# The two layers of an attention-and-ELU network on scaled float16 pairs, its first 384 tokens on whole float32 operands

## The chip, the cores and the metric

The kernel runs on one core of one Trainium2 chip, in one launch. The metric is the time of an execution on the device in microseconds; the number given for a kernel is the median of several runs. Engines are named as in the profile: PE is the matrix engine (PEld its weight loads), DVE the vector engine, ACT the scalar engine, POOL the general engine (GpSimd), SP the engine that issues the DMAs.

## What is computed

Causal attention with a decay, for 8 batch elements, 8 heads, 576 tokens and a head size of 64, then two dense layers with an ELU between them on the 4608 tokens of width 512 (2048 hidden units). The reference, cut to what matters:

```python
scores = scale * np.matmul(q, k.transpose(0, 1, 3, 2))
s_pos = np.maximum(s, 0.0)
cum = np.cumsum(s_pos, axis=-1)
bias = -(cum[:, :, :, None] - cum[:, :, None, :])
scores = np.where(causal, -1000000000.0, scores + np.minimum(bias, 0.0))
scores = scores - np.max(scores, axis=-1, keepdims=True)
attn = np.exp(scores)
attn = attn / (np.sum(attn, axis=-1, keepdims=True) + 1e-09)
attn_out = np.matmul(attn, v)
...
x = np.ascontiguousarray(attn_out.transpose(0, 2, 1, 3)).reshape(B * S, H * D)
...
h = x @ w_in
g = np.where(h > 0.0, h, alpha * (np.exp(np.minimum(h, 0.0)) - 1.0))
return (g @ w_out).astype(np.float32)
```

The scale is 1/8, alpha is 1, x is 4608 x 512, w_in 512 x 2048, w_out 2048 x 512. Here s, q, k and v are float32. The two weight matrices arrive with eight bytes an element, and the kernel turns them into float32 on the chip (lines 541 to 552).

## The kernel before, in words

**The planner.** The order of the work is not written out by hand. Every operation is registered with `op` (lines 112 to 152): a priority, one or more ways to do it (an engine and an assumed cost in nanoseconds), what it reads and what it writes. `issue` (lines 161 to 269) then repeats one step until all is issued: among the operations whose inputs are done it takes the one that can start first on its assumed clock, and among equals the one with the lowest priority number, on the engine that would finish it first. Each engine carries out its list in that order, and so does SP with its DMAs. A tile's buffer is one of a few slots under a tag, and a slot is given out in the order in which the tiles were registered.

**Attention.** It is worked through in pieces (lines 1278 and 1279): first the tokens 0 to 319 of the batch elements 0 to 2 ("low" units, lines 608 to 735, twelve of them, on whole float32 operands with transposes on PE), then the elements 3 to 7 with all 576 tokens, then the tokens 320 to 575 of the elements 0 to 2. Beyond the low units there is a unit for each head (`prepare`, `scoring`, `weighing`, lines 737 to 1083) and one for each pair of heads' first 64 tokens. Scores come from float32 operands split in two rounded parts (L882), the softmax goes through DVE (L885), ACT (L890) and DVE again, the probabilities are split into two float16 parts (L935 to L943), turned by a DMA (L369) and multiplied with V in three parts, which PE reads as the upper halves of float32 words (L1013). V is loaded in `values` (lines 845 to 856), or at line 636 for a low unit. The result of each pair of heads goes to a buffer in HBM, `x_dram`.

**The two layers.** The tokens are taken in the order in which attention finishes them, in twelve chunks of 384. Counted from 0, chunk 0 holds the element 0's low tokens and 64 of element 1; chunks 2, 5 and 8 are the first to need the elements 3, 5 and 7; the last two hold the late tokens of the elements 0 to 2. `load_x` (line 1145) loads x of a chunk, transposed, and `moe_chunk` (line 1157) does the rest. Every operand is split into a rounded part (`rounded`, line 372, type float32r, read by PE in one pass) and the rest (`rest`, line 384), so that a product takes three matmuls: high times high, high times low, low times high. That holds for x (lines 1161 to 1167), for both weight matrices (`load_unit`, lines 525 to 562, in 32 pieces of 128 x 512) and for the hidden values. For each of the 16 blocks of 128 hidden units:

- `hidden` (line 1172): 4 x 3 matmuls of 384 columns into PSUM (L1178);
- ACT takes the exponential (L1186); DVE or ACT takes min(.,1) - 1 or its negative (L1195, L1191); DVE joins it with max(h, 0) in PSUM (L1200); ACT or DVE writes the rounded copy (L394, L395); DVE writes the rest (L1203);
- `project` (line 1207), one block later: 3 x 3 matmuls of 512 columns onto three accumulators of 128 tokens (L1216).

At a chunk's end the accumulators are copied out (line 1250) and stored.

**Priorities and slots around the change.** The layers' work on the side engines has priority -1000 plus the chunk's number, ahead of attention; their matmuls have 10000 plus the chunk's number, behind attention. The weights' pieces have `W0 + WD * f` (45 + 5f), among attention's units, which count up in steps of 10 for the low units and 5 after them. A piece as it arrives takes 4 KB of a partition, in one of two slots of the tag "io" or, until x of chunk 0 is split, one of the two slots "xx" of the split x. Its split form stays in its own tile (`w_in_f`, `w_out_f`) for the whole kernel.

## Time and profile before

| | |
|---|---|
| runs, median | 1125.65 us (1124.69 to 1129.84, 3 runs) |
| profiled execution, first to last instruction (its span, the one time that the page gives for it) | 1121.7 us |
| instructions in it | 19900 |
| PE busy | 1098.8 us, 6069 matmul records |
| DVE, ACT, POOL busy | 842.3, 627.1, 448.5 us |
| moved by DMA | 156.52 MB, 140 GB/s mean |
| first matmul of the layers | at 87.15 us |
| last write of x to HBM issued | at 968.9 us |

The profile is one execution, taken by the hardware. Its page gives the busy time of each engine, the granted clock of PE in tenths of full speed, and the chain of work that ended last. The groups' rows read: line, engine, operation, output<-inputs, partitions x elements of output and inputs, count | busy us, mean ns of one | idle time of the engine just before them, and what ended it. PEld rows are the weight loads, which run beside the matmuls. A matmul's duration includes filling and draining the array, so consecutive ones overlap, and the time that one takes from the next is the distance of their starts. In a timeline the columns are start (us), length (us), engine, line, operation; equal neighbours are put in one row with their count. A tile's rows give minimum, median and maximum length in ns and the first and last start.

### The profile page before, as it was taken

How to read it: one execution, taken by the hardware profiler on the slowest of the kernel's cores; microseconds unless marked ns; L12 is line 12 of the kernel's file. 1: busy time of each engine (PE TensorE's matmuls, PEld its weight loads, DVE VectorE, ACT ScalarE, POOL GpSimd, SP SyncE). 2: the span in 40 equal slices, each digit the busy share in tenths (PEclk: the TensorE clock that was granted, in tenths of full speed). 3: DMA queues.
4: the chain of work that ended last, by engine and by line, in shares of the span. 5: the costliest groups of instructions: out<-in, count | busy, mean ns of one | idle time of the engine just before them, and what ended most of it. 6: DMA issues, size and time to landing. Idle time of an engine off the chain costs nothing.

```text
span 1121.7 us, 19900 instructions
## 1 busy us (share of the span) xinstructions
PE 1098.8 (98%) x6069; PEld 955.5 (85%) x6069; DVE 842.3 (75%) x2133; ACT 627.1 (56%) x1525; POOL 448.5 (40%) x657
## 2 busy tenths in 40 slices
PE   8999999999999999999999999999999999999998
PEld 7779888888888888888888888888888888899997
DVE  6888999778888887677887887788888888422322
ACT  5887666455556655555565555555655556433433
POOL 7663573345436234344333533445444433100000
PEclk9999999999999999999999999999999999999999
DMA  6976788567666855666755656667787687210000
GB/s 171 274 196 203 183 206 191 124 141 167 154 127 143 175 126 127 153 141 139 158 117 122 162 136 138 145 131 177 167 185 165 138 191 144 51 57 1 29 1 28
DMA packets 341689, 156.52 MB, mean 140 GB/s; under 512 B 266424, under 2 KB 320464, under 8 KB 341584
## 3 DMA queue, kind: packets, MB, share of 16 engines
q1 hardware_dynamic: 341584, 155.27, 59.4%
q8 instruction: 48, 0.79, 0.3%
q14 instruction: 57, 0.47, 0.1%
HBM read 79.66 MB, written 19.32 MB: 88 GB/s over the span
## 4 chain that ended last, share of the span: by engine, by line
PE 73%; DVE 4%; DMA 3%; issue 1%; POOL 1%; ACT 1%; SPq 1%; POOLq 0%; DVEq 0%; ACTq 0%
PE o L1216 29%; PE h L1178 29%; PE av L1013 8%; PE sc L882 6%; DVE p L943 1%; DMA T<-p 1%; DMA stq<-in_qT_dram 1%; DVE p L885 1%; DMA q<-qs 0%; DMA vs<-in_vb_dram 0%; DVE h L1200 0%; DVE xl L387 0%; DMA out_dram<-ost 0%; DMA x_dram<-x 0%; DVE qs L387 0%
## 5 line engine op out<-in xcount | busy, mean ns | idle before, releaser
L1178 PE MATMUL h<-xh,wi 128*128 128x384 f32 x1536 | 444.6, 339 | 1.1 <-DVE gl L1203 1.1
L1216 PE MATMUL o<-wo,gh 128*128 128x512 f32 x1152 | 362.1, 395 | 0.1
L1178 PEld LDWEIGHTS h<-xh,wi 128*128 128x128 f32 x1536 | 282.6, 188 | 9.3 <-DVE gl L1203 2.4
L1178 PE MATMUL h<-xl,wi 128*128 128x384 f32 x768 | 258.4, 336 | 0.0
L1216 PEld LDWEIGHTS o<-wo,gh 128*128 128x128 f32 x1152 | 207.0, 188 | 27.4 <-DVE mn L885 0.5
L1216 PE MATMUL o<-wo,gl 128*128 128x512 f32 x576 | 227.3, 395 | 0.9 <-DVE gl L1203 0.9
L1200 DVE SCALAR_TENSOR_TENSOR h<-h,g 128x384 f32<-128x384 f32 x192 | 107.8, 561 | 121.6 <-ACT g L1191 120.1
L1186 ACT ACTIVATE g<-h 128x384 f32<-128x384 f32 x192 | 94.1, 490 | 175.4 <-PE h L1178 166.0
L890 ACT ACTIVATE p<-p,mn 128x192 f32<-128x192 f32 (+1 forms) x232 | 144.9, 625 | 72.2 <-DVE mn L885 69.1
L943 DVE SCALAR_TENSOR_TENSOR p<-p,sm,p 128x512 f16<-128x512 f32 (+3 forms) x239 | 170.6, 741 | 8.1 <-POOL p L935 4.9
L1178 PEld LDWEIGHTS h<-xl,wi 128*128 128x128 f32 x768 | 144.4, 188 | 6.8
L935 POOL TENSOR_SCALAR p<-p,sm 128x512 f16<-128x512 f32 (+3 forms) x125 | 87.8, 709 | 134.8 <-DVE sm L896 51.8
L394 ACT CAST gh<-h 128x384 fp32r<-128x384 f32 x175 | 83.5, 477 | 86.7 <-DVE h L1200 85.4
L1203 DVE TENSOR_TENSOR gl<-h,gh 128x384 fp32r<-128x384 f32 x192 | 105.8, 551 | 32.8 <-ACT gh L394 31.7
L1216 PEld LDWEIGHTS o<-wo,gl 128*128 128x128 f32 x576 | 108.0, 188 | 25.2 <-DVE gl L1203 1.3
L885 DVE CUSTOM_DVE_ANT_0 p<-sc,maskw 128x192 f32<-128x192 f32 (+1 forms) x232 | 109.7, 482 | 24.9 <-PE sc L882 21.1
L1013 PEld LDWEIGHTS <-vs 128*128 128x128 bf16 x896 | 79.7, 98 | 49.7 <-issue 13.9
L1013 PE MATMUL av<-T,vs 128*128 128x256 f16 (+5 forms) x896 | 119.2, 285 | 2.8 <-DMA T<-p 2.1
L388 POOL TENSOR_TENSOR vs<-vs 128x320 f32<-128x320 f32 x72 | 60.4, 839 | 124.6 <-DMA vs<-in_vb_dram 71.1
L882 PE MATMUL sc<-kh,qs 128*128 128x192 f32 (+2 forms) x272 | 87.2, 325 | 2.1 <-DVE mn L885 1.8
L882 PE MATMUL sc<-k,q 128*128 128x192 f32 (+2 forms) x272 | 83.8, 312 | 1.4 <-POOL k L388 0.9
L1191 ACT ACTIVATE g<-g 128x384 f32<-128x384 f32 x138 | 72.5, 525 | 4.2
(149 smaller groups left out, 1368.7 us busy)
## 6 DMA issues: line engine op xcount, KB each, us to landing
stk<-in_kT_dram SPq DMA_DIRECT2D x64, 288.0 KB
vs<-in_vb_dram SPq DMA_DIRECT2D x64, 160.0 KB
stq<-in_qT_dram SPq DMA_DIRECT2D x40, 256.0 KB
w_i<-in_w_in_dram SPq DMA_DIRECT2D x16, 512.0 KB
w_o<-in_w_out_dram SPq DMA_DIRECT2D x16, 512.0 KB
out_dram<-ost SPq DMA_DIRECT2D x32, 256.0 KB
x_dram<-x_None SPq DMA_DIRECT2D x20, 288.0 KB
q<-qs SPq DMA_DIRECT2D x40, 128.0 KB
```

Of the source, the lines that this page charges most:

```text
L394: ("ACT", act_c(n), lambda: act.copy(dst(), src())),
L882: pe_.matmul(view(sc.v[:, :cw]), l, r, start=n == 0, stop=n == len(pairs) - 1)
L885: op(prio, [("DVE", 84 + dve_p(cw), lambda i=i, sc=sc: dve.tensor_tensor_reduce(pt.v[:, i * cw : (i + 1) * cw], sc.v[:, :cw], mv(i * cw, c ...
L890: op(prio, [("ACT", 480 + w / 1.2, lambda: act.activation(pt.v[:, :w], pt.v[:, :w], AF.Exp, bias=mn.v[:, n - 1 : n], scale=-1.0, accum_out ...
L935: ("Pool", 160 + 1.04 * n, lambda part=part: pool.tensor_scalar(part(t16, 0), own(part), sm.v[:, r], 1.0, ALU.mult, ALU.mult)),
L943: ("DVE-SB", dve_2(n), lambda part=part: dve.scalar_tensor_tensor(part(t16, 1), own(part), sm.v[:, r], part(t16, 0), ALU.mult, ALU.subtract)),
L1013: op(prio, [("PE", cost, lambda m=m, operands=operands, rows=rows: pe_.matmul(av.v[:rows, dst], *operands(), start=first and m == 0, stop= ...
L1178: pe_.matmul(hp.v[:, :TC], w_in_f[f].v[:, part, c * P : (c + 1) * P], xx.v[:, c, :TC], start=(c == 0 and m == 0), stop=(c == NCB - 1 and m ...
L1186: op(side, [("ACT", act_c(TC), lambda: act.activation(g.v[:, :TC], hp.v[:, :TC], AF.Exp))], [hp], [g])
L1200: op(side, [("DVE", dve_p(TC), lambda: dve.scalar_tensor_tensor(hp.v[:, :TC], hp.v[:, :TC], 0.0, g.v[:, :TC], ALU.max, join[0]))], [g], [hp])
L1203: op(side, [("DVE", dve_p(TC), lambda: dve.tensor_tensor(gl.v[:, :TC], hp.v[:, :TC], gh.v[:, :TC].bitcast(F32), ALU.subtract))], [hp, gh], ...
L1216: pe_.matmul(acc[i].v, g.v[:, tb], w_out_f[f].v[:, part], start=(f == 0 and m == 0), stop=(f == NF - 1 and m == 2),)
```

## The change

- **Scales.** For the two weight matrices, for V of the low units together, and for V of every later group of a batch element, the largest absolute value is found on chip: `peak` reduces a tile to one number for each partition (on DVE, or for a weight piece on ACT with an accumulator), and `scales_of` takes the largest over the columns, stores 128 numbers to HBM, loads all of them back into every partition, reduces again, and makes a power of two from the exponent bits. `scales_of` is called nine times: once for the weights with the low V, eight times for the groups. V bounds x, since x is a mean of V's rows.
- **Chunks 1 to 11.** x, the weights and the hidden values are scaled by these powers of two and split into a float16 part and a float16 rest. The three matmuls for each product stay; their operands are float16. The hidden value stays scaled in PSUM: ACT takes the exponential with the scale undone, DVE multiplies by the scale and takes the larger of the two (`max` in place of the sum), the float16 part is a copy times 2**-22, and the rest follows on DVE. The output copy undoes the scale. `chunk_scales` works out five numbers for a chunk with small DVE operations.
- **Chunk 0.** It uses the float32 words of the weights, x as loaded and the hidden value as one float32 tile: one matmul where there were three, no split of x, weights or hidden value.
- **Weights.** A piece's float32 words get a tile of their own (`w_in_f`, `w_out_f`, half the size of before); the float16 pairs (`w_parts`) are made after the scales, by `split_unit`, at priority -500 + f. The rest of a weight is made on DVE only (before: DVE or POOL). Arriving pieces have the two slots "io" alone. The step between the pieces' priorities, `WD`, is 3 (5 before).
- **x.** The split x takes half the space; x of chunk 0 uses the tiles of the later split x instead of "io" slots.

The diff, cut to its core:

```diff
-W0, WD = 45, 5
+W0, WD = 45, 3
...
+    def peak(prio, n, src, reads, at, axis=mybir.AxisListType.X, aside=None, also=()):
+        col = slice(at, at + 1)
+        ways = [("DVE-SB", 100 + 1.04 * n, lambda: dve.tensor_reduce(
+            peaks.v[:, col], src(), axis, ALU.max, apply_absolute_value=True))]
+        if aside is not None:
+            ways.append(("ACT", 480 + n / 1.2, lambda: act.activation(
+                aside(), src(), AF.Abs, accum_out=peaks.v[:, col])))
+        op(prio, ways, reads, [(peaks, at), *also])
...
+    def scales_of(prio, spans, dst):
...
+        used = [(peaks, m) for at, k in spans for m in range(at, at + k)]
+        op(prio, [("DVE-SB", 30.0 + 70 * n, largest)], used, [own])
+        load(prio, lambda: aside.v.rearrange("n p -> p n"), lambda: own.v, [own], [aside], P * n * 4)
+        load(prio, lambda: every.v, lambda: aside.v.rearrange("n p -> (n p)").partition_broadcast(P),
+             [aside], [every], P * P * n * 4)
+        op(prio, [("DVE-SB", 300.0 + 130 * n, exponents)], [every], [own, (scales, dst)])
...
+    def weight_scales():
+        scales_of(-600, [(A_IN, NF + 1), (A_OUT, NF + 1), (A_LOW, N_CUT * NP + 1)], 0)
...
-        raw = plan.buf(sb, shape, dtype, f"w_{n}", tag="io", bufs=N_IO,
-                       others=[("xx", 2, 0)] + [(t, 1, 0) for t in later])
...
+            raw = plan.buf(sb, [P, 512, 2], U32, f"w_{n}", tag="io", bufs=N_IO,
+                           others=[(w.key[1], 1, 0) for w in w_parts[:N_STAGE]], always=True)
...
-        rounded(prio, 512, lambda: parts.v[:, 0], value, [words], [(parts, 0)])
-        rest(prio, 512, lambda: parts.v[:, 1], value, lambda: parts.v[:, 0].bitcast(F32),
-             [words, (parts, 0)], [(parts, 1)])
+        peak(prio, 512, lambda: value.v, [value], (A_IN, A_OUT)[kind] + f,
+             aside=(lambda: raw.v[:, :, 0].bitcast(F32)) if wide else None, also=[(raw, 0)] if wide else [])
+
+    def split_unit(f, kind, value):
+        prio, col, parts = -500 + f, slice(kind, kind + 1), w_parts[f]
+        scaled(prio, 512, lambda: parts.v[:, kind, 0], lambda: value.v, lambda: scales.v[:, col],
+               [value, (scales, 0)], [(parts, (kind, 0))])
+        op(prio, [("DVE-SB", dve_2(512), lambda: dve.scalar_tensor_tensor(
+            parts.v[:, kind, 1], value.v, scales.v[:, col], parts.v[:, kind, 0], ALU.mult, ALU.subtract))],
+           [value, (scales, 0), (parts, (kind, 0))], [(parts, (kind, 1))])
...
+        peak(prio, n * D, values, [(u.vs, 0), (u.vs, 2)], A_LOW + b * NP + j, mybir.AxisListType.XY)
...
+        peak(prio, m * D, lambda: u.vs.v[:, :m, 0], [(u.vs, 0)], first + 2 * u.j + u.h, mybir.AxisListType.XY)
+        if (u.j, u.h) == (NP - 1, 1):
+            scales_of(prio, [(first, H + 1)], 4 + at)
...
-    xh, xl = (plan.buf(sb, [P, NCB, TMAX], F32R, n, tag="xx", bufs=2) for n in ("xh", "xl"))
+    xh, xl = (plan.buf(sb, [P, NCB, TMAX], F16, n, tag=n) for n in ("xh", "xl"))
...
+        native = ch == 0
...
+        def hidden_native(f):
+            hp = plan.buf(ps, [P, TMAX], F32, f"h_{ch}_{f}", tag="h", bufs=N_H)
+            for c in range(NCB):
+                op(main, [("PE", pe4(TC), lambda c=c: pe_.matmul(
+                    hp.v[:, :TC], w_in_f[f].v[:, c * P : (c + 1) * P], xc[c // 2].v[:, c % 2, :TC],
+                    start=c == 0, stop=c == NCB - 1))],
+                   [(xc[c // 2], (c, t)) for t in offs] + [w_in_f[f]], [hp])
...
             op(side, [("DVE", dve_p(TC), lambda: dve.scalar_tensor_tensor(
-                hp.v[:, :TC], hp.v[:, :TC], 0.0, g.v[:, :TC], ALU.max, join[0]))], [g], [hp])
-            psum_copy(side, TC, lambda: gh.v[:, :TC], lambda: hp.v[:, :TC], [hp], [gh])
-            op(side, [("DVE", dve_p(TC), lambda: dve.tensor_tensor(
-                gl.v[:, :TC], hp.v[:, :TC], gh.v[:, :TC].bitcast(F32), ALU.subtract))], [hp, gh], [gl])
+                hp.v[:, :TC], g.v[:, :TC], by(2 if sign[0] else 1), hp.v[:, :TC], ALU.mult, ALU.max))],
+               [g, cs], [hp])
+            op(side, [
+                ("ACT", act_c(TC), lambda: act.activation(
+                    gg.v[:, 0, :TC], hp.v[:, :TC], AF.Copy, scale=2.0**-DOWN)),
...
+            ], [hp], [(gg, 0)])
             op(side, [("DVE", dve_p(TC), lambda: dve.scalar_tensor_tensor(
+                gg.v[:, 1, :TC], hp.v[:, :TC], 2.0**-DOWN, gg.v[:, 0, :TC], ALU.mult, ALU.subtract))],
+               [hp, (gg, 0)], [(gg, 1)])
...
-                            acc[i].v, g.v[:, tb], w_out_f[f].v[:, part],
+                            acc[i].v, gg.v[:, g, tb], w_parts[f].v[:, 1, part],
...
+    weight_scales()
+    for f in range(NF):
+        split_unit(f, 0, w_in_f[f])
+        split_unit(f, 1, w_out_f[f])
```

More of the change, by code (lines that the diff above doesn't have):

```diff
@@ L853, in values @@
                  [(u.vs, 0)], HB * D * 4)
+        at = groups.index((u.b, u.blocks[0] > 0))
+        first = A_GROUP + at * (H + 1)
+        peak(prio, m * D, lambda: u.vs.v[:, :m, 0], [(u.vs, 0)], first + 2 * u.j + u.h, mybir.AxisListType.XY)
+        if (u.j, u.h) == (NP - 1, 1):
+            scales_of(prio, [(first, H + 1)], 4 + at)
         for i in range(2):
@@ L1229, in moe_chunk @@
                 steps.pop(0)()
-            hidden(f)
+            (hidden_native if native else hidden)(f)
             for step in steps:
@@ L1239, in moe_chunk, with output @@
         following = after()
+        def output(n, dst, src, reads, writes, only=None):
+            if native:
+                psum_copy(side, n, dst, src, reads, writes, only)
+                return
+            ways = [
+                ("ACT", act_c(n) + 90, lambda: act.activation(dst(), src(), AF.Copy, scale=by(4))),
+                ("DVE", dve_p(n), lambda: dve.tensor_scalar(dst(), src(), by(4), None, ALU.mult)),
+            ]
+            op(side, [w for w in ways if only is None or w[0] in only], reads + [cs], writes)
         for i in range(NTB):
```

176 lines of the change are left out of this document (129 added, 47 removed).

## The prediction

> **What bounds the kernel now.** I read the page first, for the busy shares and the granted clock:
>
> ```profile
> span 1121.7 us, 19900 instructions
> PE 1098.8 (98%) x6069; PEld 955.5 (85%) x6069; DVE 842.3 (75%) x2133; ACT 627.1 (56%) x1525; POOL 448.5 (40%) x657
> PEclk9999999999999999999999999999999999999999
> PE 73%; DVE 4%; DMA 3%; issue 1%; POOL 1%; ACT 1%; SPq 1%; POOLq 0%; DVEq 0%; ACTq 0%
> ```
>
> The matrix engine is busy for 98% of the span at full clock, and 73% of the chain that ended last is its own work. A shorter kernel therefore needs less matmul time, as long as the matmuls keep finding their inputs ready. Busy time overlaps from one matmul to the next, so I take real costs from starts, in a timeline of the matrix engine in the last stage, where only the two layers run:
>
> ```profile
> 1002.35 0.33 PE L1178 MATMUL h<-xh,wi 128*128 128x384 f32 x1
> ...
> 1004.46 0.63 PE L1216 MATMUL o<-wo,gh 128*128 128x512 f32 x2
> ...
> 1006.54 0.33 PE L1178 MATMUL h<-xh,wi 128*128 128x384 f32 x1
> ```
>
> One block of 128 hidden units is 12 matmuls of 384 columns in 2.11 us (176 ns each) and 9 of 512 columns in 2.08 us (231 ns each): 4.19 us. A chunk has 16 blocks, 67.0 us; twelve chunks are 804 us, over 70% of the span. What else loads the stages is in the table by stretches:
>
> ```profile
> 87.00:970.00 883.00, 873.82 (x4868) 757.80 (x4866) 724.35 (x1816) 506.04 (x1206) 386.32 (x518) 1.00 0.67 152
> 970.00:1122.00 152.00, 147.57 (x739) 133.14 (x737) 47.32 (x83) 56.49 (x114) 4.80 (x6) 1.00 0.06 22
> ```
>
> After the stretch's length the columns are PE, PEld, DVE, ACT and POOL. Until 970 us attention and layers run together and DVE is 724/883 = 82% busy; then only the layers are left and DVE is at 31%. So the matrix engine sets the end, with DVE next in the long first stretch; in the last, with ACT at 56/152 = 37%, somewhat shorter blocks meet no new bound.
>
> **The eleven float16 chunks.** The matmul count stays (192 of 384 columns and 144 of 512 a chunk); only the operands become float16. The trace has matmuls with a float16 moving operand in attention, L1013; here beside the layers' in the groups by line and shape:
>
> ```profile
> L1178 PE MATMUL h<-xh,wi 128*128 128x384 f32 x1536 | 444.6, 339 | 1.1 <-DVE gl L1203 1.1
> L1178 PE MATMUL h<-xl,wi 128*128 128x384 f32 x768 | 258.4, 336 | 0.0
> L1216 PE MATMUL o<-wo,gh 128*128 128x512 f32 x1152 | 362.1, 395 | 0.1
> L1013 PE MATMUL av<-T,vs 128*128 128x512 f16 x120 | 32.8, 382 | 2.5 <-DMA T<-p 2.1 <-issue 0.3
> L1013 PE MATMUL av<-T,vs 128*128 128x448 f16 x120 | 29.2, 352 | 0.0
> L1013 PE MATMUL av<-T,vs 128*128 128x320 f16 x120 | 22.8, 299 | 0.0
> L1013 PE MATMUL av<-T,vs 128*128 128x256 f16 x216 | 27.8, 274 | 0.3 <-DMA x_dram<-x 0.3
> ```
>
> At 512 columns float16 takes 382 ns against 395, 13 less. At 384, midway between 320 and 448, it would take 325.5 against 338 (two thirds of 339, one of 336), 12.5 less. Both kinds carry the same fill, so the difference is one of spacing. A chunk saves 192 x 12.5 + 144 x 13 = 4.27 us, eleven save 47 us. For the bounds, spacing itself. In the late units 14 such matmuls follow one another:
>
> ```profile
> 777.88 1.46 PE L1013 MATMUL av<-T,vs 128*128 128x256 f16 x14
> 779.18 0.38 PE L882 MATMUL sc<-kh,qs 128*128 128x288 f32 x1
> ```
>
> By the code these are nine of 256 columns, three of 192 and two of 64, 3008 columns in 1.30 us, 0.432 ns a column: 166 and 221 ns, 10 less each, 37 us in all. That charges a long matmul with the fixed cost of short ones, so it is the low end. The slope (382 - 274)/256 = 0.422 ns a column without fixed cost gives 162 and 216 ns, 4.85 us a chunk, 53 us: the high end. I take 47, the comparison at equal size. The Trainium skill, "TensorE: Matmul & The Clock Gate", section "Back-to-back issue gap", gives N/2.4 + 2.5 ns for a warm stream; by it the saving would be 11 x (192 x 13.3 + 144 x 15.3) ns = 52 us, inside these bounds.
>
> **The first chunk on whole float32.** It now has one matmul where three were: 64 of 384 and 48 of 512 columns. Whole float32 matmuls are in the first stage (timeline, then groups):
>
> ```profile
> 44.51 1.24 PE L882 MATMUL sc<-kl,ql 128*128 128x320 f32 x4
> 45.59 0.60 PE L688 MATMUL avl<-tl,vs 128*128 128x128 f32 x3
> L882 PE MATMUL sc<-kl,ql 128*128 128x320 f32 x44 | 15.0, 434 | 0.0
> L688 PE MATMUL avl<-tl,vs 128*128 128x256 f32 x48 | 12.5, 383 | 0.0
> ```
>
> L688 shows 48 records at 256 columns where the code issues 24 (12 units, two heads), so each such matmul is two records. Four records of 320 columns take 1.08 us, 0.844 ns a column each: 648 ns for a matmul of 384, 864 for one of 512. The chunk takes 64 x 0.648 + 48 x 0.864 = 82.9 us, 16 more than 67.0. The slope of the two rows, 51 ns over 64 columns, gives 11 more; four times today's 176 and 231 ns gives 22 more. I take 16.
>
> Its matmuls need no split of x. Today the split ends at 80.1 and the first matmul starts at 87.15; the last load of x was issued at 75.81:
>
> ```profile
> 75.81 0.32 SPq L364 DMA_DIRECT2D xc<-x_dram  x1
> L388 POOL TENSOR_TENSOR xl<-xc,xh x2: 997/1012/1027, 73.4 to 79.1; 128x384 fp32r<-128x384 f32 x2
> 87.15 0.42 PE L1178 MATMUL h<-xh,wi 128*128 128x384 f32 x1
> 170.15 0.33 PE L1178 MATMUL h<-xh,wi 128*128 128x384 f32 x1
> ```
>
> The layers' matmuls stand behind attention's in the planner, and 7 us lay between the split's end and the start, so I take 2 us earlier (0 to 8).
>
> **The weights.** They are still loaded and turned into float32 as before, but rounding and rest now wait for the scales, which wait for all 32 maxima. Chunk 0 needs only the float32 words. Today chunk 0 lasts 83.0 us (87.15 to 170.15), 16 more than its layers' 67; with 82.9 it ends near 85 + 82.9 + 16 = 184. The rows of the weights' tiles, of two small DMAs in the chain, and of two DVE groups:
>
> ```profile
> L364 SPq DMA_DIRECT2D w_o<-in_w_out_dram x16: 328/426/734, 15.3 to 158.8; - x16
> L550 DVE SCALAR_TENSOR_TENSOR w_o<-w_o x16: 661/688/1427, 25.5 to 165.5; 128x512 uint32<-128x512 uint32 x16
> 272.31 3.15 DMA q<-qs
> ...
> 374.17 2.20 DMA q<-qs
> L395 DVE COPY ost<-o 128x512 f32<-128x512 f32 x7 | 4.8, 690 | 3.8 <-PE o L1216 3.8
> L895 DVE TENSOR_SCALAR sm<-sm 128x4 f32<-128x4 f32 x40 | 8.2, 204 | 4.5 <-ACT p L890 3.9
> ```
>
> The rows of the chain give a start and a length. The last word is done near 166.2. Then come its maximum (0.7, as L395), small DVE steps (five of 0.2, as L895, and two over more elements, 1.5 together), two small DMAs one after the other (2.2 to 3.2 each) and the first split (two steps of 0.7): about 176. Chunk 0 covers it with 8 us to spare, so I cost it at nothing. While SP holds the second small DMA until the first has landed, attention's loads and turns behind it wait as long; nine such pairs over the kernel.
>
> **DVE.** The operations of a hidden block stay one for one (exponential, minus one, join, copy, rest). Chunk 0 loses 16 rests (L1203) and two of x. New are maxima and scales. No reduction over SBUF of this kind is in the trace; nearest are:
>
> ```profile
> L885 DVE CUSTOM_DVE_ANT_0 p<-sc,maskw 128x320 f32<-128x320 f32 x52 | 25.2, 484 | 4.9 <-PE sc L882 3.5 <-ACT pl L890 0.4 <-PE trl L707 0.4
> L1203 DVE TENSOR_TENSOR gl<-h,gh 128x384 fp32r<-128x384 f32 x192 | 105.8, 551 | 32.8 <-ACT gh L394 31.7
> ```
>
> Up to the start of chunk 8 (counted from 0) that is 40 units' V x 0.48 = 19 us, 12 low units x 0.65 = 8, 32 weights x 0.69 = 22 (zero to DVE where the planner gives them to ACT), six group scales at 1.3 = 8, eight chunk scales of five small steps at 0.2 = 8; less 16 x 0.55 + 2 x 0.55 = 10. About +55 us on an engine that is 82% busy, 33 if ACT takes the maxima. What can suffer is the arrival of x. Chunks that begin a batch element have the least time:
>
> ```profile
> 770.44 0.48 SPq L364 DMA_DIRECT2D xc<-x_dram  x1
> 793.57 0.78 DVE L380 TENSOR_SCALAR xh<-xc 128x384 fp32r<-128x384 f32 x1 [0.61 <-PE h L1178]
> 799.34 0.33 PE L1178 MATMUL h<-xh,wi 128*128 128x384 f32 x1
> ```
>
> The last x of chunk 8 is loaded by 770.44 + 3.15 = 773.6 and first split at 793.6, 20 us later. In the changed kernel it is wanted at 793.6 + 14 - 7 x 4.27 = 777.7: 4 us of the 20 are left. The weights' rests are moved: 32 x 0.69 = 22 us, on DVE alone now, that fall after 176 and go ahead of attention by their priority, while attention makes the x of chunk 2:
>
> ```profile
> 250.77 0.36 SPq L364 DMA_DIRECT2D xc<-x_dram  x1
> 256.25 0.53 ACT L378 ACTIVATE xh<-xc 128x384 fp32r<-128x384 f32 x1 [0.83 <-PE h L1178]
> ```
>
> That x landed by 253.9 and is wanted at 256.3 + 14 - 4.27 = 266: 12 us cover over half of the 22, and if all of it reached attention 0.75 x 10 = 8 us would be lost here instead of at chunk 8.
>
> For the forecast I let a fifth of DVE's addition reach attention, 11 us, since DVE idles 18% of that stretch and a maximum is in nobody's way except on DVE itself. That leaves the x of chunk 8 7 us late; attention fills about a quarter of it (chunks 1 to 7 took (799.34 - 170.15)/7 = 89.9 us each, 67 of it the layers'), so the loss is 5 us (0 if nothing is passed on, 0.75 x (30 - 4) = 19 if over half is).
>
> **Sum.** 1121.7 - 47 + 16 - 2 + 5 = 1093.7 us of span; the median of the runs, 1125.65, is 3.95 above the profiled span, so 1097.6, rounded to **1098 us**.
>
> **Rivals.** *Attention becomes the bound (slower).* DVE's additions delay attention until x of chunk 8 is late and the matrix engine stands. Slower by 0.5% is 1131.3; without lateness the sum is 1092.7, so 38.6 us of standing decide. With a quarter filled that is 51 us of lateness, a delay of 55: all of DVE's addition passed on. At 62 us of delay the time is 1092.7 + 0.75 x 58 = 1136. For it: DVE's 82%, and L547 below. Against it: DVE's idle time, and that a starved matrix engine sends DVE no layer work, so attention catches up.
>
> ```profile
> L547 DVE TENSOR_SCALAR w_i<-w_i x16: 409/428/1310, 18.0 to 158.0; 128x512 uint32<-128x512 uint32 x16
> ```
>
> The same instruction takes 428 or 1310 ns (minimum, median, maximum). The Trainium skill, "SBUF — State Buffer", section "SBUF: two separate sides", says that DVE and GpSimd take their shared port pair as an exclusive lock for a whole instruction; the spread of this row agrees, and rests put on DVE alone would meet it too. Chance 0.09.
>
> *The scales come late.* Only two staging buffers are left for weights, where four served until x was split. A pair of loads came every (158.8 - 15.3)/15 = 9.6 us; at 12 us a pair the last is issued at 195, 36 us later than now, chunk 1 waits until 176 + 36 = 212, 28 us after chunk 0, three quarters of it lost: 1098 + 21 = 1119. Against it: a staging buffer is now free before rounding and rest, two steps earlier. Chance 0.10.
>
> *Float16 streams no faster.* Then 1121.7 + 16 - 2 + 3.95 = 1140. The L1013 rows speak against it; chance 0.02.
>
> *Float16 streams far faster.* If float16 matmuls overlapped so deeply that the layers needed less time than DVE, DVE would set it: 842 + 55 us of work at nine tenths is about 1000 us. The 0.432 ns a column above contradict it; chance 0.01. The Trainium skill, "TensorE: Matmul & The Clock Gate", section "Back-to-back issue gap", states such a sustained rate, 131 ns at 512 columns; the trace disagrees with 382 ns against 395 and the 1.30 us.
>
> **How the numbers follow.** The forecast has 0.78. Its range: 1121.7 - 53 + 16 - 4 + 0 + 3.95 = 1085 to 1121.7 - 37 + 16 - 2 + 19 + 3.95 = 1122. I give 1084 to 1122; outside lie the slower rivals (0.11), part of the late scales (0.03), the fast one and a lower tail (0.06). A measurement tells 0.5% from nothing, 1120.0 to 1131.3. Faster: 0.74 of the forecast, 0.06 of the late scales, 0.01: 0.81. Same: 0.04 and 0.04, 0.08. Slower: 0.11.
>
> **What would show it.** Right: chunk spacing in the last stage near 16 x 3.92 = 62.7 us; two float32 records of about 490 or 600 ns for each matmul of chunk 0 (434 - 270 = 164 of fill, and 324 or 432), the chunk near 99 us; the first float16 matmul near 185 with no stand before it; DVE near 900 us. Wrong: blocks of 4.19 us in the tail; a gap before chunk 1, ended by a scale or a split; idle PE before chunks 2, 5 or 8, ended by a split of x whose load came late, with DVE above 90% in the stretch before.

## The result and the profile after

The changed kernel takes 1180.22 us (median of 4 runs, 1175.88 to 1182.96), the kernel before 1127.38 us in the same comparison (4 runs, 1124.69 to 1129.84): a ratio of 1.0467, 95% interval 1.0432 to 1.0503. It is 4.7% slower; 1098 us and a range up to 1122 had been forecast.

The page of the changed kernel: span, busy times and granted clock.

```profile
span 1178.0 us, 19825 instructions
PE 1083.7 (92%) x5941; PEld 643.6 (55%) x5941; DVE 880.8 (75%) x2263; ACT 642.4 (55%) x1521; POOL 486.0 (41%) x719
PEclk9999998898899999998999989999998998999999
```

The matrix engine has less to do (1083.7 us busy, 1098.8 before), yet its share fell from 98% to 92%, and the clock row, all nines before, has eights. The page's chain of work is followed back only over the last 142 us, so its shares say little here. The float16 matmuls themselves are as forecast. PE in the last stage (timeline), and the groups by line and shape:

```profile
1121.24 0.33 PE L1331 MATMUL h<-xh,wp 128*128 128x384 f16 x1
...
1123.19 2.11 PE L1368 MATMUL o<-wp,gg 128*128 128x512 f16 x9
1125.13 0.33 PE L1331 MATMUL h<-xh,wp 128*128 128x384 f16 x1
```

```profile
L1331 PE MATMUL h<-xh,wp 128*128 128x384 f16 x1408 | 394.9, 331 | 30.9 <-DVE gg L1349 21.0 <-DVE sm_None L974 9.8
L1368 PE MATMUL o<-wp,gg 128*128 128x512 f16 x1584 | 392.7, 385 | 4.2 <-ACT gg L1344 4.2
L1315 PE MATMUL h<-x,wi 128*128 128x384 f32 x128 | 46.5, 490 | 0.0
L1360 PE MATMUL o<-wo,gg 128*128 128x512 f32 x96 | 45.8, 597 | 3.1 <-DVE gg L1321 3.1
```

Twelve matmuls of 384 columns take 1.95 us (162.5 ns each), nine of 512 take 1.94 (215.6): a block of 3.89 us, where the forecast had 3.92 and the kernel before 4.19. Chunk 0 has two float32 records for each matmul, of 490 and 597 ns. What is new stands behind the bars: idle time of PE, ended by DVE. The waits of PE, DVE and SP, each from the changed kernel's list of waits (total us, times, longest):

```profile
PE h L1331 <- DVE gg L1349: 21.0, 13, 6.5
PE h L1331 <- DVE sm_None L974: 9.8, 1, 9.8
PE av L1092 <- DVE wp L635: 9.3, 1, 9.3
```

```profile
DVE own L582 <- DMA every<-aside: 26.5, 6, 9.1
DVE own L582 <- DMA stq<-in_qT_dram: 9.6, 1, 9.6
```

```profile
SPq L373 <- DMA aside<-own: 34.4, 7, 7.1
```

DVE stands for the number that comes back from HBM (`every`), and SP for the store ahead of it (`aside`). The nearest look at one such trip is the chain near the end (start, length, what), with PE's own rows for it below:

```profile
1054.46 7.73 DMA aside<-own
1062.21 5.68 DMA every<-aside
...
1069.54 0.62 DVE h L1340
1070.16 0.02 issue
1070.19 0.50 ACT gg L1344
1070.69 0.05 issue
1070.73 3.57 PE o L1368 x9
1074.30 2.35 PE h L1331 x12
1076.64 1.94 PE o L1368 x9
```

```profile
1066.23 0.33 PE L1331 MATMUL h<-xh,wp 128*128 128x384 f16 x1
1070.73 3.57 PE L1368 MATMUL o<-wp,gg 128*128 128x512 f16 x9 [4.17 <-ACT gg L1344]
...
1076.48 0.81 PE L1368 MATMUL o<-wp,gg 128*128 128x512 f16 x3
```

Two small DMAs take 13.4 us, where the forecast had 4.4 to 6.4. DVE's reduction of `every` (L582) stands in DVE's fixed order ahead of the join of a hidden block (L1340), so the join is late, and PE stands for 4.17 us. Then the pause costs a second time: the next nine matmuls need 3.57 us where the same nine need 1.94 a few lines on, and the twelve after them 2.35 instead of 1.95. By the starts, from 1070.73 to 1076.48, the 21 take 5.75 us in place of 3.89, which is 1.9 more, and the row of the stretches has a granted clock (the first figure after the engines) of 0.83:

```profile
1065.00:1075.00 10.00, 5.83 (x22) 2.29 (x21) 4.09 (x13) 2.46 (x5) 0.00 (x0) 0.83 0.10 32
```

The Trainium skill, "TensorE: Matmul & The Clock Gate", section "HAM oscillation — how this bites in real kernels", warns of pauses of PE above about 3.4 us, behind which the clock is lowered for a while. This pause agrees with it: it is 4.17 us long, and from 1071.6 to 1075.0 us the granted clock is 0.50.

For an account of the whole span I add up, over all matmul records, the pauses between one's end and the next one's start ("standing") and the remaining time from the first to the last start ("work"). Before: 16.7 standing and 1098.4 work. After: 88.2 and 1083.3. So 1121.7 + 71.5 - 15.1 = 1178.1, against a measured span of 1178.0. Before, no pause is longer than 3 us; after, eight are, 50.7 us together. Seven of the eight begin 4 to 12 us behind the issue of one of the nine stores; the other, 3.7 us at 212.6 us, doesn't.

### The profile page after: what moved, and what is told of

The parts are those of the page before. It is cut to its first block, busy times and chain, and to the rows that moved or that the text cites. A ratio compares the mean times of both kernels' runs of the same rounds, so it can differ in the third digit from the quotient of the medians.

```text
span 1178.0 us, 19825 instructions
## 1 busy us (share of the span) xinstructions
PE 1083.7 (92%) x5941; PEld 643.6 (55%) x5941; DVE 880.8 (75%) x2263; ACT 642.4 (55%) x1521; POOL 486.0 (41%) x719
## 5 line engine op out<-in xcount | busy, mean ns | idle before, releaser
L1331 PE MATMUL h<-xh,wp 128*128 128x384 f16 x1408 | 394.9, 331 | 30.9 <-DVE gg L1349 21.0
L1368 PE MATMUL o<-wp,gg 128*128 128x512 f16 x1584 | 392.7, 385 | 4.2 <-ACT gg L1344 4.2
L1331 PEld LDWEIGHTS <-wp 128*128 128x128 f16 x2112 | 199.9, 99 | 183.8 <-issue 44.2
L1368 PEld LDWEIGHTS <-gg 128*128 128x128 f16 x1584 | 148.8, 99 | 161.8 <-issue 10.3
L1331 PE MATMUL h<-xl,wp 128*128 128x384 f16 x704 | 232.7, 331 | 0.4 <-DVE xl L1284 0.4
L1295 ACT ACTIVATE g<-h,cs 128x384 f32<-128x384 f32 x176 | 102.0, 579 | 161.8 <-PE h L1331 156.8
L1340 DVE SCALAR_TENSOR_TENSOR h<-g,cs,h 128x384 f32<-128x384 f32 x176 | 108.4, 616 | 79.8 <-ACT g L1302 78.7
L1344 ACT ACTIVATE gg<-h 128x384 f16<-128x384 f32 x163 | 79.7, 489 | 113.4 <-DVE h L1340 111.5
L1349 DVE SCALAR_TENSOR_TENSOR gg<-h,gg 128x384 f16<-128x384 f32 x176 | 96.9, 551 | 28.0 <-ACT gg L1344 26.5
L1018 ACT ACTIVATE p<-p,sm 128x512 f16<-128x512 f32 (+3 forms) x94 | 53.0, 581 | 15.2 <-DVE sm L975 6.7
```

Source lines behind the costliest of these rows:

```text
L1295: op(side, [("ACT", act_c(TC) + (0 if native else 90), lambda: act.activation(g.v[:, :TC], hp.v[:, :TC], AF.Exp, scale=1.0 if native else ...
L1331: pe_.matmul(hp.v[:, :TC], w_parts[f].v[:, 0, part, c * P : (c + 1) * P], xx.v[:, c, :TC], start=(c == 0 and m == 0), stop=(c == NCB - 1 a ...
L1340: op(side, [("DVE", dve_p(TC), lambda: dve.scalar_tensor_tensor(hp.v[:, :TC], g.v[:, :TC], by(2 if sign[0] else 1), hp.v[:, :TC], ALU.mult ...
L1349: op(side, [("DVE", dve_p(TC), lambda: dve.scalar_tensor_tensor(gg.v[:, 1, :TC], hp.v[:, :TC], 2.0**-DOWN, gg.v[:, 0, :TC], ALU.mult, ALU. ...
L1368: pe_.matmul(acc[i].v, gg.v[:, g, tb], w_parts[f].v[:, 1, part], start=(f == 0 and m == 0), stop=(f == NF - 1 and m == 2),)
```

## The experiments

All times are medians; each kernel was compared with the kernel before in its own runs (1126.1 to 1127.6 us there). Standing and work are those of the profiled execution.

| kernel | time, us | ratio to before (95%) | standing | work | pauses over 3 us |
|---|---|---|---|---|---|
| before | 1125.65 | | 16.7 | 1098.4 | 0 |
| changed | 1180.22 | 1.0467 (1.0432 to 1.0503) | 88.2 | 1083.3 | 8 |
| e1 constants, no maxima | 1109.6 | 0.9842 (0.9825 to 0.9858) | 39.6 | 1066.5 | 1 |
| e2 constants, maxima kept | 1117.22 | 0.9922 (0.9894 to 0.995) | 36.1 | 1070.5 | 1 |
| e3 planner told of the delay | 1178.31 | 1.0436 (1.038 to 1.0493) | 85.7 | 1084.9 | 8 |
| e4 row stores | 1134.3 | 1.0066 (1.0051 to 1.0081) | 52.1 | 1073.0 | 4 |
| e5 trips through PE | 1596.55 | 1.4159 (1.4138 to 1.418) | 325 | 1264.8 | 40 |
| e6 store that nobody reads | 1167.73 | 1.037 (1.0337 to 1.0403) | 71.5 | 1086.0 | 7 |
| e7 same, 512 bytes apart | 1120.84 | 0.9947 (0.9933 to 0.9961) | 42.6 | 1070.5 | 0 |
| e8 = e1, chunk 0 on float16 | 1111.24 | 0.9861 (0.9848 to 0.9875) | 49.6 | 1052.6 | 4 |
| e9 groups through PE | 1140.29 | 1.0128 (1.0103 to 1.0153) | 56.4 | 1079.5 | 5 |
| e10 = e6 on ACT's queue | 1160.43 | 1.0302 (1.0275 to 1.0328) | 72.0 | 1082.1 | 6 |
| e11 = e4, weights' scales constant | 1131.77 | 1.0017 (0.9993 to 1.0041) | 50.0 | 1073.6 | 2 |
| e12 = e4, splits behind | 1138.42 | 1.0104 (1.0073 to 1.0135) | 58.9 | 1071.2 | 1 |

**e1 and e2: constants for the scales.** e1 has neither maxima nor round trips; e2 keeps the maxima, and does nothing with them.

```diff
 def scales_of(prio, spans, dst):
+    return
...
-    op(-8, [("Pool-M", 60.0, lambda: pool.memset(scales.v, 1.0))], [], [scales])
+    op(-8, [("Pool-M", 300.0, constants)], [], [scales])   # 2**16, 2**17, 2**15, 2**-17
...
 def peak(...):
+    return                                                 # e1 alone
```

> This kernel leaves out finding the scales: no maxima, no round trip through HBM; constants of the size that these inputs give stand in their place, so its time is that of the float16 layers and the float32 first chunk alone. Theory T1 (the nine round trips, with DVE and SP waiting in order for their DMAs, make the matrix engine stand): 1121.7 - 50 + 16 = 1088 of span, about 1092 us, 1085 to 1105, at full clock. Rival T2 (the maxima on DVE delay attention): the same, about 1092. Rival T3 (the layers in their new form, or the order that the planner finds for them, make it stand): 1150 or more.

> All maxima are still taken (on DVE or ACT), but nothing is made of them: no reduction of the maxima, no DMAs, constants as scales. T1 (round trips): within 10 us of the kernel without maxima, about 1098 us. T2 (maxima on DVE delay attention): most of the loss stays, 1150 to 1175 us. T3: 1150 or more, as without maxima.

Measured: 1109.6 and 1117.2 us. e1 is some 5 us above T1's range, e2 within the 10 us that T1 allowed for the maxima; T2 and T3 are far off. The float16 pairs and the float32 chunk make the kernel 1.6% faster, the maxima give 7.6 us of it back (by the medians; the profiled executions are only 0.5 apart), and everything else, 1180.2 - 1117.2 = 63 us, lies in the nine round trips and in what waits for their scales. DVE's additional maxima are a small part.

**e3: the planner is told how long the trips take.** Its assumed delay, 1.8 us for every DMA, becomes 9.5 us for the store and 5.5 us for the load; nothing else changes.

```diff
-    load(prio, ..., [own], [aside], P * n * 4)
-    load(prio, ..., [aside], [every], P * P * n * 4)
+    load(prio, ..., [own], [aside], P * n * 4, lag=9500.0)
+    load(prio, ..., [aside], [every], P * P * n * 4, lag=5500.0)
```

> The whole computation; only the planner is told a longer delay for the two small DMAs of a round trip (9.5 and 5.5 us after the issue, near what the trace of the changed kernel shows, in place of 1.8), so that it puts other work ahead of what waits for them. T1a (the loss is in-order waiting behind an operation issued too early): most of the standing goes, 1100 to 1125 us. T1b (the small store to HBM itself holds up the DMAs behind it, whoever waits): 1145 to 1170 us. T2, T3: no change, 1180 us.

Measured: 1178.3 us, no better, and outside the ranges of both T1a and T1b. What it did reach is telling. These are SP's whole wait for such stores in its trace, and the longest of PE's waits:

```profile
SPq L378 <- DMA aside<-own: 4.1, 1, 4.1
PE h L1331 <- DVE gg L1349: 34.2, 15, 7.8
```

SP's 34.4 us of waiting (and 5.5 more before its turns) are 4.1 now, and in the list of waits DVE's 36 us for `every` (26.5 + 9.6, of which the profile puts the 9.6 down to another load) are gone. The time is the same. So the engines that stand for the trip, which the chain shows so plainly, are not what it costs: take their waits away, and the loss comes out elsewhere; PE's wait for the hidden values, 21.0 us in the changed kernel, is 34.2 here.

**e4: whole rows to HBM.** The 128 maxima, one in each partition, first go by DMA into one SBUF row; the row is stored as 512 neighbouring bytes by one partition.

```diff
-    load(prio, lambda: aside.v.rearrange("n p -> p n"), lambda: own.v, [own], [aside], P * n * 4)
+    row = plan.buf(sb, [1, n * P], F32, f"row_{dst}", tag=f"row{n}")
+    for m in range(n):
+        load(prio, lambda m=m: row.v[:, m * P : (m + 1) * P], lambda m=m: own.v[:, m : m + 1], [own], [(row, m)], P * 4)
+    load(prio, lambda: aside.v.rearrange("(o n) p -> o (n p)", o=1), lambda: row.v, [row], [aside], P * n * 4)
```

> The whole computation; the 128 maxima are first brought into one row of SBUF by a DMA, the row is then stored to HBM as one piece of 512 bytes, and loaded back as before: one more DMA in a row, but none that writes 4 bytes at a time to HBM. T1b (the 4-byte writes to HBM hold up the DMAs): the time from the first of these DMAs to the load of all maxima falls from about 9 to 5 us and the time to 1130 to 1155 us. T1a (in-order waiting for whatever number of DMAs): as long or longer, 1175 to 1200 us.

Measured: 1134.3 us, in T1b's range. A third DMA in each trip makes the kernel 46 us faster, and the trip itself shorter: the last one takes 7.8 us from its first issue to DVE's reduction, 13.5 in the changed kernel. That points to the form of the store, which the next three runs test.

**e6, e7 and e10: the store by itself.** Scales are constants again; the maxima are reduced and stored, but nobody reads the store or waits for it. In e7 the 128 numbers lie 512 bytes apart in HBM. In e10 ACT issues the stores, on its own DMA queue.

```diff
-aside = plan.buf(dram, [n, P], F32, f"aside_{dst}")
+aside = plan.buf(dram, [n, P, 128], F32, f"aside_{dst}")                        # e7
...
-load(prio, lambda: aside.v.rearrange("n p -> p n"), lambda: own.v, ...)
+load(prio, lambda: aside.v.rearrange("n p q -> p n q")[:, :, 0], lambda: own.v, ...)   # e7
+op(prio, [("ACT", 100.0, lambda: act.dma_start(aside.v.rearrange("n p -> p n"), own.v), ...)])  # e10
...
-load(prio, lambda: every.v, ...)
-op(prio, [("DVE-SB", 300.0 + 130 * n, exponents)], ...)                         # all three
```

> All maxima, their reduction to 128 numbers and the store of these, 4 bytes from each partition, into 512 neighbouring bytes of HBM, nine times; nothing reads what is stored, nobody waits for it, and constants stand in as scales. T1b (the store holds up the DMAs behind it): most of the loss is there though nobody waits, 1150 to 1180 us. T1a (waiting for the round trip is the loss): 1117 to 1125 us, as without the store.

> As the kernel that only stores, but the 128 stored numbers lie 512 bytes apart in HBM. If the hold-up comes of many writers of 4 bytes in one small stretch of memory: 1117 to 1125 us. If it comes of a write of 4 bytes as such: the same as with neighbouring numbers.

> As the kernel with maxima, reduction and the 4-byte store that nobody reads (constants stand for the scales; 1167.7 us), but the nine stores are issued by ACT on its own DMA queue in place of SP's. Left out: reading the maxima back and using them. Theory A (the small pieces hold up the DMA engines or the place in HBM itself, so that any transfer of that time suffers, whatever its queue): 1160 to 1175. Theory B (only what stands behind the store in the same queue is held up, in the order of the queue): 1117 to 1128, as with the stored numbers 512 bytes apart (1120.8), and SP's loads land after their usual 2 to 3 us while the store is under way.

Measured: 1167.7, 1120.8 and 1160.4 us, each in a range that had been given: of T1b (e6), of "many writers of 4 bytes in one small stretch of memory" (e7) and of theory A (e10). Nine stores of 128 x 4 bytes (three times 128 in that of the weights) that nobody waits for cost 50.5 us over e2 where their targets are neighbours, and 3.6 us where they lie apart. Here are the ten microseconds behind the stores of the eight groups, in the stretches of e6, of e7 and of e10 (the first two of e6 and e7, the first of e10, and the sum of each; the last two figures of a row are the busy share of the DMA engines and the GB/s that they moved):

```profile
223.60:233.60 10.00, 4.33 (x23) 2.33 (x21) 6.42 (x17) 4.95 (x14) 3.27 (x7) 0.78 0.70 82
362.20:372.20 10.00, 7.41 (x41) 4.12 (x39) 6.27 (x18) 4.67 (x12) 4.51 (x8) 1.00 0.46 75
...
sum 80.00, PE 60.99 PEld 34.91 DVE 43.80 ACT 27.89 POOL 23.18; mean PE 7.62 PEld 4.36 DVE 5.47 ACT 3.49 POOL 2.90
```

```profile
218.90:228.90 10.00, 7.49 (x41) 3.72 (x38) 7.52 (x22) 6.42 (x17) 4.00 (x8) 1.00 0.81 135
354.80:364.80 10.00, 10.00 (x58) 5.95 (x56) 8.60 (x25) 6.90 (x18) 5.14 (x8) 1.00 0.58 111
...
sum 80.00, PE 75.58 PEld 43.72 DVE 66.19 ACT 51.02 POOL 38.34; mean PE 9.45 PEld 5.47 DVE 8.27 ACT 6.38 POOL 4.79
```

```profile
226.40:236.40 10.00, 6.27 (x38) 3.57 (x37) 5.52 (x13) 4.13 (x9) 2.00 (x5) 1.00 0.42 82
...
sum 80.00, PE 64.40 PEld 36.97 DVE 48.82 ACT 33.69 POOL 15.08; mean PE 8.05 PEld 4.62 DVE 6.10 ACT 4.21 POOL 1.88
```

The DMA engines are as busy, and move half as much: over the eight stretches the mean share is 0.69 in e6 and 0.65 in e7, the mean rate 67 and 130 GB/s, in e10 0.78 and 81. Most of it falls between 2 and 8 us behind the issue, at 47 GB/s in e6 and 134 in e7; in the 6 us ahead of the issue both have 138. Attention's loads come late, ACT, DVE and POOL run dry, and PE works 61.0 of the 80 us instead of 75.6. In the whole trace of e6 PE has seven pauses over 3 us, and all seven begin 2 to 9 us behind one of the stores; e7 has none. That it is no matter of the order within one queue is what e10 shows: with the stores on another queue the loads of SP's queue suffer as well. The changed kernel's trace has the same in SP's timeline, where the loads behind the store are issued at once, but POOL gets one of them, `stv_None`, only at 265.49 (9 us after its issue; the last row is POOL's), and the second small DMA is issued at 265.21:

```profile
255.92 0.38 SPq L373 DMA_DIRECT2D aside<-own  x1
256.35 0.42 SPq L373 DMA_DIRECT2D stv_None<-in_vb_dram  x1
256.82 0.42 SPq L373 DMA_DIRECT2D stk<-in_kT_dram  x1
257.29 0.58 SPq L373 DMA_DIRECT2D k<-aux_dram  x2
257.96 0.63 SPq L373 DMA_DIRECT2D k2s<-aux_dram  x1
265.21 0.34 SPq L373 DMA_DIRECT2D every<-aside  x1
265.49 0.24 POOL L385 TENSOR_SCALAR vs_None<-stv_None 128x64 fp32r<-128x64 f32 x1 [12.30 <-DMA stv_None<-in_vb_dram]
```

The Trainium skill, "DMA: Bandwidth & Descriptors", section "Specifications", says that below 512 bytes a transfer becomes a read, a change and a write. The size alone doesn't part e6 from e7, whose pieces are 4 bytes in both; that 128 such pieces share one stretch of 512 bytes does. A queueing of these rewrites at one place would fit, but no run here shows it directly, and no distance between 4 and 512 bytes was tried.

**e8: is the float32 chunk worth its 16 us?** It is e1 with chunk 0 on float16 pairs too, whose x as loaded gets tiles of its own.

```diff
-        native = ch == 0
+        native = False
```

> Constants as scales, no maxima, no round trips (finding the scales is left out), and chunk 0 on float16 pairs too, as the other eleven. The matmuls of chunk 0 take 62 us in place of 82: if the matrix engine sets the time, 20 us less than the kernel with constants and a float32 first chunk (1109.6), so about 1090 us. If the side engines set the pace of the first 300 us (weights, splits, attention), the gain is under 8 us: 1102 to 1112.

Measured: 1111.2 us, against 1109.6, in the range given for side engines that set the pace of the first 300 us. PE's work falls by 13.9 us and its standing grows by 10.0, 3.8 less in the profiled spans and nothing in the medians. But the reason given isn't the one that the trace shows: only some 2.5 of the 10.0 us come before 300 us. Chunk 1 begins at 176.0 us in place of 212.7, and still attention's last x is written at 990.1, in e1 at 991.1. So 14 us of matmuls more or less at the start change nothing that these runs tell; why the lead is lost later stays open.

**e5: trips through PE.** No DMA at all: PE turns the maxima, DVE reduces the row, and a small product with ones brings the result into all partitions.

```diff
+    tr, bc = (plan.buf(ps, [P, 512], F32, f"{m}_{dst}", tag="a", bufs=N_A) for m in ("trs", "bcs"))
...
+    op(prio, [("PE", 111.0, lambda: pe_.transpose(tr.v[:n, :P], own.v, ident))], [own], [tr])
+    op(prio, [("DVE", 650.0, exponents)], [tr], [top])
+    op(prio, [("PE", 222.0, lambda: pe_.matmul(bc.v[:, :n], ones4[:n], top.v[:n, 1:], start=True, stop=True))],
+       [top], [bc])
...
```

> The whole computation, the scales found on chip, but without any DMA: the 128 maxima of a scale are turned into a row by a transpose on PE, reduced on DVE, made a power of two, and spread to all partitions by a small float32 matmul with ones. T1b (the 4-byte store to HBM and what it holds up is the loss): a few us above the kernel with all maxima and no round trip (1117), so 1112 to 1128 us, not slower than the kernel before. If on the other hand any way of finding the scales in the middle of the work costs its waits on DVE: 1140 to 1175 us.

Measured: 1596.6 us, far outside both ranges: a kernel with another trouble. The first float16 matmul comes at 890 us (PE's timeline):

```profile
890.49 0.48 PE L1336 MATMUL h<-xh,wp 128*128 128x384 f16 x1 [2.19 <-DVE xh L399]
```

The trip of the weights is registered behind all of attention, and the slots of a tag are given out in the order of registration: its PSUM slot came up only when attention's score banks were through. So the run says nothing about trips through PE, only about where they may be registered.

**e9: the groups' trips through PE, in attention's order.** The eight groups' trips are registered right behind their unit's steps; the weights' trip is that of e4.

```diff
-            scales_of(prio, [(first, H + 1)], 4 + at)
+            trips.append((prio, [(first, H + 1)], 4 + at))
...
+            while trips:
+                scales_pe(*trips.pop())
             behind = weighed(u)
```

> The whole work is done, with two other round trips for the scales. The eight groups' scales no longer touch a DMA: the 128 maxima are turned by PE (one transpose), DVE reduces them to one exponent, and a one-row product with ones brings it into all partitions; the trip is registered right behind the steps of its unit, so that its two PSUM slots come in attention's own order. The weights' trip goes through one SBUF row and a store of whole rows, as in the version that took 1134.3 us. Theory (the 4-byte stores are the cost, and what is left of 1134.3 above the 1117.2 us of the kernel with maxima but constants is the length of the DMA trips): 1117 to 1126, PE standing 36 to 46 us, faster than both kernels. Rival (waiting for any true scale costs what the row version lost, since attention's work on V and x is then bound to the trip however short it is): 1130 to 1138. Second rival (the trip's slots disturb attention's score banks, as in the version of 1596.6 us on a smaller scale): over 1140, with gaps of PE before scores.

Measured: 1140.3 us, outside the theory's 1117 to 1126. It is just above the range of the rival "waiting for any true scale costs" (1130 to 1138) and just within that of the second (over 1140), whose sign, gaps of PE before scores, isn't there: PE's waits for DVE before scores are 4.0 us, 7.5 in e4. The trips are short, from a transpose at 257.2 us to the scales at 263.2, and 1011.6 to 1013.7 at the end. So shorter trips did not take away what is left in e4 above the 1117.2 us of e2. The standing between 100 and 300 us is what both keep. The stretches of e2, e4 and e9 from 100 to 300 us, whose first figure after the length is PE's busy time:

```profile
100.00:300.00 200.00, 193.12 (x875) 110.44 (x874) 174.56 (x428) 117.36 (x285) 103.50 (x140) 0.98 0.69 168
```

```profile
100.00:300.00 200.00, 177.90 (x750) 97.84 (x750) 168.77 (x391) 106.77 (x246) 89.94 (x117) 0.94 0.57 140
```

```profile
100.00:300.00 200.00, 179.18 (x761) 98.76 (x760) 168.49 (x399) 109.52 (x256) 88.45 (x117) 0.95 0.59 146
```

**e11 and e12: the lump of the weights' splits.** In e4 and e9 all 32 pieces wait for one scale, then their splits fill DVE and others from 175 us on. e11 gives the weights and the low V constants, so that a piece is split as it arrives; e12 keeps the scales, and moves the splits behind attention's units of that time.

```diff
-        scales_of(-600, [(A_IN, NF + 1), (A_OUT, NF + 1), (A_LOW, N_CUT * NP + 1)], 0)   # e11: not done, constants
...
-        prio, col, parts = -500 + f, slice(kind, kind + 1), w_parts[f]
+        prio, col, parts = 150 + 2.5 * f, slice(kind, kind + 1), w_parts[f]              # e12
```

> The version with row stores (1134.3 us), but the scales of the weights and of the low V are constants, so that a weight piece is split as it arrives; the groups' scales are found on chip as before, with eight row trips. Left out: reducing the 32 maxima of the weights and of the low V to a scale. In the row version, and in the one whose groups go through PE (1140.3), the last x of element 3 is written at 276 us, against 246 us in the kernel with constants (1117.2), and PE stands 22 us between 100 and 300 us against 6.8. Theory (the lump of weight splits after the one late scale, on DVE ahead of attention, is most of what is left): 1116 to 1123, the last x of element 3 near 246, PE standing 36 to 42 us, 8 or less of it between 100 and 300 us. Rival (the groups' trips are what is left): 1129 to 1136, with the standing between 300 and 1100 us.

> The row version with the whole work done; only the priority of the weights' splits is changed, from -500 + f (ahead of attention) to 150 + 2.5 f (among attention's units of that time). Theory (the lump costs because it goes ahead of attention on DVE): attention's x of element 3 comes back to 250 to 265 us and the time falls to 1118 to 1130. Rival (chunk 1 needs the 32 pieces in its own 63 us whatever the order, so that PE only waits for splits in place of attention): 1132 to 1150, with PE's waits before the hidden matmuls ended by a weight's split.

Measured: 1131.8 us (12 runs, 1123.1 to 1133.4) and 1138.4. The theory failed in both, though the lump is real: the last x of element 3 is written at 268.1 and 269.1 us, not near 246 and not by 265. The same stretch of e11 and of e12:

```profile
100.00:300.00 200.00, 191.01 (x869) 109.85 (x868) 163.46 (x398) 116.54 (x284) 91.60 (x125) 0.99 0.65 159
```

```profile
100.00:300.00 200.00, 188.77 (x852) 105.17 (x853) 174.94 (x418) 116.80 (x272) 93.07 (x124) 0.99 0.61 150
```

PE has 13 and 11 us more of work there than in e4, and the time is given back: in e11 5.9 us in the first 100 us, where the splits now stand, and 5.4 after 300; in e12 17 us after 300. Both times lie in the ranges of the rivals. That of e11, the groups' trips, has a part of its sign: PE's standing after 300 us is 26.1 us, 16.7 in e2. That of e12 hasn't: no wait of PE is ended by a weight's split. What is left of e4 above e2, 17 us, thus isn't one wait that can be taken away. The order that the planner finds is another one in each kernel, so a part of it may be no more than that. It stays open. No version with true scales beat the kernel before.

## Why the prediction was wrong, point by point

**The step that failed** is the trip of the scales, in "The weights": "two small DMAs one after the other (2.2 to 3.2 each)", and "so I cost it at nothing". Both DMAs were priced by rows of another kind (q<-qs, whole rows of columns). No row of the profile before shows a store of single numbers, and for that very operation no bound from above was given. The trip took 13 us instead of 5; but its length is not the price. The price, put at nothing in the prediction, is what one store does to the other transfers of the following eight microseconds or so: 46.9 us for nine (e6 less e7), 5.2 each. I had the number nine and the queue ("attention's loads and turns behind it wait as long"), and stopped there, without working out nine times it, and without asking what comes late after attention's loads.

**How the 82 us between 1098 and 1180 divide**, by the runs: 11.6 from the forecast to e1; 7.6 for the maxima (e2); 3.6 for reducing and storing 512 bytes apart (e7); 46.9 for storing as neighbours (e6); 12.5 for reading back and for waiting for true scales (the changed kernel). The 11.6 hide a larger miss: the 1098 holds 5 us for DVE's maxima, which e1 doesn't take, so e1 is some 17 us above what was forecast for the layers alone. A part of the store's price is the clock: PE's work is 1086.0 us in e6 and 1070.5 in e7, for the same matmuls, with a mean granted clock of 0.977 and 0.994. Seven pauses at the 1.9 us of the one shown above would make 13 of these 15.5; that is an estimate.

**Float16, -47 us, and chunk 0, +16.** Right as work: their sum, -31, is -31.9 in e1 (1066.5 against 1098.4), the block 3.89 us. That it fits so closely is in part luck: 0.30 us in each of 176 blocks are 53, not 47, and with 16 for chunk 0 that would be -37; the mean granted clock, 1.000 before, is 0.993 in e1, by estimate up to 8 us of its 1113. The Trainium skill's N/2.4 + 2.5 ns ("TensorE: Matmul & The Clock Gate", section "Back-to-back issue gap"), which that section gives for a single isolated matmul and not, as the prediction has it, for a stream, would be 162.5 and 215.8 ns. The trace has 162.5 and 215.6 in a stream, so of the bounds given the high end was nearer. Wrong as time: e1 gained 16 to 18 us of the 31.9, for standing rose from 16.7 to 39.6 us, 8.2 of it in the first 100 us. A shorter matmul stream waits more often for the side engines; the largest item of e1's list of waits of PE, the wait for the hidden value's rest, was 1.1 us before (the prediction's row of L1178):

```profile
PE h L1335 <- DVE gg L1353: 10.1, 9, 2.3
```

The sentence "somewhat shorter blocks meet no new bound" was argued from DVE's mean share in the last stage. It holds there (behind the last x PE has no pause, before and in e1), and fails in the long stretch, where DVE is at 82%.

**Chunk 0's start and end.** The first matmul was forecast near 85 and came at 83.0. But the chunk's last came at 204.5, not 184, with 14.1 us of standing between 100 and 200 us. The sign "the first float16 matmul near 185 with no stand before it" was the one named for it, and it came out wrong.

**DVE's maxima, 5 us.** e2 less e1 is 7.6 us: the size was nearly right, but by luck, for the place was not. DVE was busy for 880.8 us, not 900; 16 of the weights' maxima went to ACT; and no pause before chunk 8 was ended by a late x.

**The rivals.** "The scales come late" named the place (a pause before chunk 1: PE stood for 9.3 us from 170.7 on, until DVE's split of a weight by the profile) with the wrong cause: the staging buffers were no shortage, the last load of a weight was issued at 148.7 us, 10 earlier than before. "Attention becomes the bound" gave a slower kernel for another reason than the one that came: DVE's share of the span is 75%, as before. That a store in the trip could slow down everything else was no rival. Two conditions spoke for looking: a new kind of DMA, and a queue on which attention depends.

## What to carry to other kernels

A maximum over all partitions shouldn't leave the chip as 128 numbers of 4 bytes side by side: gather them in one SBUF row first (46 us here for nine trips), or keep them 512 bytes apart (47 us, run here only with nobody reading them back). An operation of a kind that the trace doesn't have needs an upper bound of its own, times its count, above all where it shares a resource with what feeds the bottleneck. And when a wait in the chain is taken away and the time stays (e3), the wait was a symptom; test the transfer by itself, with nobody waiting for it (e6, e7).

## What the runs showed of the hardware

- A store of 128 neighbouring 4-byte pieces halves what the DMA engines move in the ten microseconds behind its issue, 67 GB/s in e6 against 130 in e7 with the pieces apart, at busy shares of 0.69 and 0.65. With the store on another queue than the loads it is 81 GB/s (e10).
- A pause of PE costs more than its length. After 4.17 us the next 21 matmuls took 5.75 us instead of 3.89 in the changed kernel, with the granted clock at 0.50 for 3.4 us. Shorter pauses did it at times as well: after 1.96 us in e1 (at 639.5 us) the next matmuls lost 1.7 us, after others of that length nothing. In e5, where PE stood 325 us, the mean granted clock was 0.82.
- Float32 in chunk 0 costs PE 13.9 us of work and the kernel nothing that was measured (1109.6 us in e1, 1111.2 in e8).
